# Eight plain chunks instead of six, one tile pair of weight forms a chunk, and packing spread over four steps

## The chip, the cores and the metric

The kernel runs on one core of one Trainium2 chip. The core has a matrix engine (PE, with its weight loads shown as PEld), a vector engine (DVE), a scalar engine (ACT), a general engine (POOL) and a queue that issues transfers (SP). Each runs its own instructions strictly in the order in which they stand; they wait for one another by semaphores. The metric is the time of one execution in microseconds of the device. Before the change the runs shown gave 1952.1, 1952.52 and 1952.86 us.

## The reference

x has 8192 tokens of 448 values. A spectral layer (Fourier transform, a small complex MLP on four blocks of 112, inverse transform) is followed by a GEGLU layer, both behind a normalised and modulated input:

```python
x = x + ga * _A_ref(h, A_w1, A_b1, A_w2, A_b2)      # spectral layer
h = _layernorm(x, axis=-1) * (1 + cb) + sb
x = x + gb * _B_ref(h, B_w_gate, B_w_up, B_w_down)  # GEGLU

def _B_ref(x, w_gate, w_up, w_down):                # 448 -> 1792 -> 448
    return (_gelu(x @ w_gate) * (x @ w_up)) @ w_down
```

The change lies wholly in the second half, the inverse transform's last stage and the GEGLU.

## The kernel before

Up to about 386 us the kernel does the transforms and the spectral MLP and prepares weights. Then it goes through the 8192 tokens in 32 chunks of 256. For precision every operand of the GEGLU products is split into a high and a low 16-bit part, so each product is three matmuls.

**Plain chunks.** The first NSTD = 6 chunks, numbered 0 to 5, do the gate and up products plainly. A chunk has 14 steps, one for each 128 columns of the hidden layer; step k of chunk i is `gate_up(i, k)`: 20 matmuls of 256 columns on PE, and for two hidden tiles together a group of eight of half height. ACT then makes the GELU (L1154, tile gel) and DVE multiplies it with the up half out of PSUM (L1159, tile x), which frees the bank; POOL makes four sums (L1167 to L1170), ACT and DVE the high and low parts (L1178, L1179, tile ac). The eight tiles of PSUM that gate/up and the other products share turn over, so PE can be about two steps ahead of L1159. After step 2 of a chunk comes `down` of the chunk before (seven products, 147 matmuls, L1191 to L1193; its tail of additions runs on DVE and on POOL, L1205, L1206, L1234).

**The work beside them.** During chunk i the input of chunk i + 2 is made ready, in steps given by the table `hooks`: splitting the spectral data into parts (step 3: ACT, and POOL L115), the inverse (step 6: PE, L1018 to L1020), the residual (step 7: DVE L1029, POOL L1030), the statistics (8: DVE L1038, L1041), the reciprocal root (9 and 10: DVE L124 to L133), the norm (11 and 12: DVE L1067, L1068), packing (13: ACT and POOL), and in step 0 of the next chunk the transposing transfers (`turn`).

**Set chunks.** The other 26 chunks use a scheme with seven products in place of eight for gate and up, 546 matmuls of 128 columns (L1350). It needs the weights in seven sums and differences, the weight forms, again in high and low parts. They are made while the plain chunks run, for seven tile pairs (n = 0 to 6): `load_forms` fetches a pair (four transfers, tile wr), `form_sums` makes the sums on POOL (L1528 to L1532, tiles wr and wf), `forms_hi` the high parts on ACT (L1557, tile ws), `forms_lo` the low ones on DVE (L1561), and `store_forms` copies three of them (POOL, L1566) and writes the pair to memory in two parts of four transfers (L1569). The set chunks then load them part by part (`load_part`, L1269) into the four slots that the plain weights leave.

A planner sets the place of this: `plan` gives each item a due time in microseconds (33 a pair, `spots` being the expected times of a chunk's steps), and an item comes at the first spot at or after it. So the pairs do not keep step with the chunks: about 1.4 of them fall to a chunk, each in four bursts of two or three pieces on ACT and DVE.

**The passage.** The last plain chunks also pack the inputs of the first two set chunks, which is more work: sums over the two token halves (`token_sums`: DVE L1294 to L1300) and five packings (`wpack_hi` on ACT, L1321, `wpack_lo` on POOL, L1327). In the kernel before all of it comes in step 13 (`pack`). The PSUM tiles of the set chunks (`sets`) take the place of those of the plain ones, so the first set matmul waits for the last L1159.

Of the kernel before, what the change touches and what calls it, by code (L numbers as in the profile page):

```python
# [40 lines left out]
NSTD = 6  # L41
# [8 lines left out]
def spectral_geglu(ctx, tc, x, w1, b1, w2, b2, wg, wu, wd, cvec, wmod, cf1, cs2, cmi, cgm, out):  # L50
# [924 lines left out]
    with ExitStack() as cctx:  # L975
# [558 lines left out]
        def form_cuts(t, part):  # L1534

            w, r, s2 = raws[("s", t, part // 2)], raws[("w", t)], raws[("f", t)].rearrange("p (c x) -> p c x", c=3)
            tq = r[:, :, 6:7]
            cuts = [
                [(A12, 0, r[:, 0, 3:6]), (A12, 3, tq[:, 0]), (A11, 0, r[:, 0, 0:3])],
                [(S1, 0, r[:, 1, 0:3]), (S2, 0, s2)],  # L1540
                [(A22, 0, r[:, 1, 3:6]), (S4, 3, tq[:, 0]), (S4, 0, r[:, 0, 3:6])],
                [(S3, 0, s2), (A22, 3, tq[:, 1].to_broadcast([128, 2, 128]))],
            ][part]
            f0 = WPARTS[part // 2][0]

            def out(l, f, c, src):
                if c == 0:
                    return w[:, l, 0:3, f - f0]
                return w[:, l, 3, f - f0 : f - f0 + src.shape[1]]

            return [(out(0, *cut), out(1, *cut), cut[2]) for cut in cuts]

        def forms_hi(t, part):
            if part % 2 == 0:
                raws[("s", t, part // 2)] = cp2.tile([128, 2, 4, 4 - part // 2, 128], F16, tag=f"ws{part}", name="ws")
            for hi, _, src in form_cuts(t, part):
                S.activation(hi, src, AF.Copy, scale=sww)  # L1557

        def forms_lo(t, part):
            for hi, lo, src in form_cuts(t, part):  # L1560
                V.scalar_tensor_tensor(lo, src, sww, hi, op0=ALU.mult, op1=ALU.subtract)  # L1561

        def store_forms(t, part):
            w = raws.pop(("s", t, part))
            if part == 0:
                G.tensor_copy(w[:, :, 3, 0:3], w[:, :, 2, 0:3])  # L1566
# [4 lines left out]
        spots = [(0, 2.4), (1, 4.9), (2, 7.3), ("m0", 11.3), ("m1", 13.3), ("m2", 17.4)]  # L1571
        spots += [(k, 21.4 + 2.44 * (k - 2)) for k in range(3, NFT)]
        prep = {}

        def plan(us, fn, *args):
            i, r = divmod(us, 48.2)
            i, p = next(((1 + int(i), p) for p, at in spots if at >= r), (2 + int(i), 0))
            prep.setdefault((i, p), []).append((fn, *args))

        for n in range(NP):  # L1580
            for us, fn, *args in (
                (0, load_forms),
                (11, form_sums, 0),
                (11, forms_hi, 0),
                (11, forms_lo, 0),
                (14, forms_hi, 1),
                (14, forms_lo, 1),
                (17, form_sums, 1),
                (19, store_forms, 0),
                (20, forms_hi, 2),  # L1590
                (20, forms_lo, 2),
                (23, forms_hi, 3),
                (23, forms_lo, 3),
                (28, store_forms, 1),
            ):
                plan(33 * n + us, fn, n, *args)
        for n, k in enumerate((4, 7, 11, 13)):
# [4 lines left out]
            0: [(1, turn)],  # L1602
# [228 lines left out]
```

## Time and profile before

| what | value |
|---|---|
| median of the runs shown | 1952.52 us |
| the profiled execution, and its span | 1953.62 us, 1951.8 us |
| PE, DVE, ACT, POOL busy | 96%, 74%, 52%, 65% of the span |
| mean granted clock of PE | 0.981 |
| plain chunks 1 to 5 begin and end | 425.98 us and 726.77 us |
| first set chunk ends, one later one | 778.05 us, 46.20 us long |

A row of the busy time by stage gives the stretch in us from the span's start, its length, then for each engine the busy time and the number of instructions, and last the granted clock of PE, the share of DMA time and GB/s. A row of a timeline gives start, length, engine, line, operation, the tiles written and read, and in brackets how long the engine stood idle before it and who ended that. A row of the groups gives busy time and mean length in ns, then the idle time before the group's instructions by who ended it. Matmuls overlap, so a matmul's length is more than what it adds.

### The profile page before, as it was taken

To read this page: it belongs to the slowest core of one execution; us is meant where nothing else is said; L and a number is where in the kernel's file an instruction comes from. 1 tells how busy PE (TensorE), PEld (TensorE's weight loads), DVE (VectorE), ACT (ScalarE), POOL (GpSimd) and SP (SyncE) were. 2 spreads that over 40 slices of the span, in tenths; PEclk is the share of its full clock that TensorE was granted. 3 is DMA by queue.
4 is the path that set the end of the run, shared out by engine and by line. 5 is a ranking of instruction groups with operands and counts; after the bars stand their busy time and mean duration, and the time that the engine had idled before them with its cause. 6 is when DMAs were issued, how large, how long until landed. Compare 5 with 4: busy or idle time off the path is not lost.

```text
span 1951.8 us, 57569 instructions
## 1 busy us (share of the span) xinstructions
PE 1867.3 (96%) x23808; PEld 1767.8 (91%) x23808; DVE 1451.8 (74%) x2919; ACT 1010.4 (52%) x1879; POOL 1276.7 (65%) x1633
## 2 busy tenths in 40 slices
PE   7899999899989859999999999999999999999998
PEld 3599999777878749999999999999999999999998
DVE  8677788786756666777777777777777777777745
ACT  5687788553433424555444444455455555545443
POOL 3157655256767666777777677777777777777633
PEclk9899999999989979999999999999999999999999
DMA  9999777654354466666666665666666655666561
GB/s 354 317 280 261 193 191 190 175 137 108 94 132 107 96 218 164 173 175 177 178 182 178 172 165 163 163 168 182 173 182 173 162 163 163 178 171 182 147 173 53
DMA packets 395454, 342.14 MB, mean 175 GB/s; under 512 B 113332, under 2 KB 373560, under 8 KB 395192
## 3 DMA queue, kind: packets, MB, share of 16 engines
q1 hardware_dynamic: 395192, 338.47, 62.8%
q8 instruction: 186, 3.05, 0.7%
q14 instruction: 76, 0.62, 0.1%
HBM read 254.33 MB, written 60.10 MB: 161 GB/s over the span
## 4 chain that ended last, share of the span: by engine, by line
PE 71%; DVE 10%; POOL 6%; DMA 5%; issue 3%; ACT 2%; SPq 2%; ACTq 0%; POOLq 0%; DVEq 0%
PE set L1350 40%; PE pdn L1193 5%; PE pdn L1191 5%; PE pdn L1192 5%; PE ps L210 2%; PE set L1193 2%; PE set L1191 2%; PE set L1192 2%; DVE y L471 1%; PE pgu L1118 1%; DMA wr<-in_B_w_up 1%; DVE ws L1561 1%; POOL x L1167 1%; DMA raw<-in_B_w_up 1%; SPq L1569 1%
## 5 line engine op out<-in xcount | busy, mean ns | idle before, releaser
L1350 PE MATMUL set<-nt,wk 128*128 128x128 f16 x14196 | 805.9, 219 | 7.5 <-ACT sb L1378 3.5
L1350 PEld LDWEIGHTS <-wk 128*128 128x128 f16 x14196 | 798.4, 98 | 12.9 <-issue 10.7
L1193 PE MATMUL pdn<-wd,ac 128*128 128x224 f16 x1190 | 308.3, 259 | 3.0 <-DVE ac L1179 1.8
L1191 PE MATMUL pdn<-wd,ac 128*128 128x224 f16 x1190 | 308.5, 259 | 2.3 <-DVE u L1227 0.7
L1192 PE MATMUL pdn<-wd,ac 128*128 128x224 f16 x1190 | 308.2, 259 | 0.0
L1399 ACT ACTIVATE gl<-c,dg 128x384 f32<-128x384 f32 x182 | 112.2, 616 | 275.5 <-DVE c L1393 274.4
L1425 DVE SCALAR_TENSOR_TENSOR ac<-x,sa_act,ac 128x896 f16<-128x896 f32 x182 | 229.6, 1261 | 16.1 <-ACT ac L1415 16.0
L1118 PE MATMUL pgu<-nt,wk 128*128 128x256 f16 (+1 forms) x1848 | 214.1, 282 | 16.2 <-DVE x L1159 16.2
L1118 PEld LDWEIGHTS <-wk 128*128 128x128 f16 (+1 forms) x1848 | 175.3, 101 | 54.7 <-issue 30.3
L1234 POOL TENSOR_TENSOR o<-u,p 128x224 f32<-128x224 f32 x32 | 21.0, 658 | 285.2 <-DVE u L1233 285.2
L1403 DVE TENSOR_TENSOR x<-c,gl 128x384 f32<-128x384 f32 x182 | 191.5, 1052 | 18.5 <-ACT gl L1399 18.5
L1167 POOL TENSOR_TENSOR x<-x 128x128 f32<-128x128 f32 x223 | 126.9, 569 | 118.7 <-DVE x L1159 50.2
L1415 ACT ACTIVATE ac<-x,sa_act 128x896 f16<-128x896 f32 x182 | 188.2, 1034 | 3.4 <-DVE x L1170 0.4
L1170 POOL TENSOR_TENSOR x<-x 128x128 f32<-128x128 f32 x223 | 175.5, 787 | 0.0
L1191 PEld LDWEIGHTS <-ac 128*128 128x128 f16 x1568 | 153.4, 98 | 6.6 <-issue 5.2
L1193 PEld LDWEIGHTS <-ac 128*128 128x128 f16 x1568 | 153.4, 98 | 4.2 <-DVE ac L1179 2.5
L1387 DVE TENSOR_TENSOR c<-set,sb 128x512 f32<-128x512 f32 x182 | 124.5, 684 | 43.6 <-PE set L1350 43.6
L1192 PEld LDWEIGHTS <-ac 128*128 128x128 f16 x1568 | 153.4, 98 | 1.8 <-issue 1.8
L1169 POOL TENSOR_TENSOR x<-x 128x128 f32<-128x128 f32 x223 | 147.5, 661 | 0.0
L1378 ACT COPY sb<-set 128x512 f32<-128x512 f32 x182 | 105.0, 577 | 54.5 <-PE set L1350 54.5
L471 DVE SCALAR_TENSOR_TENSOR y<-pm,t 64x224 f32<-64x224 f32 x256 | 99.5, 389 | 39.0 <-ACT t L463 35.1
L115 POOL TENSOR_TENSOR yl<-y,yh 128x448 fp32r<-128x448 f32 x63 | 76.6, 1215 | 73.7 <-ACT yh L113 58.1
(323 smaller groups left out, 3993.5 us busy)
## 6 DMA issues: line engine op xcount, KB each, us to landing
wk<-wk SPq DMA_DIRECT2D x82, 1024.0 KB, 5.6
wk<-wk SPq DMA_DIRECT2D x82, 768.0 KB, 10.5
tr<-td SPq DMA_DIRECT2D x64, 224.0 KB, 4.7
vd<-us SPq DMA_DIRECT2D x64, 224.0 KB, 3.1
xx<-in_A_x SPq DMA_DIRECT2D x32, 448.0 KB
v<-vd SPq DMA_DIRECT2D x63, 224.0 KB, 6.3
out<-x SPq DMA_DIRECT2D x31, 448.0 KB, 5.3
xt<-in_A_x SPq DMA_DIRECT2D x15, 896.0 KB, 16.3
```

The lines of the kernel that those rows point to most:

```text
L1118: T.matmul(pgu[i, t, q][:, pr * H : (pr + 1) * H], ws[rows, n, w, tw], nts[i][rows, tn, :], start=start, stop=stop, skip_group_check=True,)
L1167: e.tensor_tensor(s1, a21, a22, ALU.add)
L1169: e.tensor_tensor(s3, a11, a21, ALU.subtract)
L1170: e.tensor_tensor(s4, a12, s2, ALU.subtract)
L1191: T.matmul(ps, ac[:, 0, ka], w[:, 0, kb], start=n == 0, stop=False)
L1192: T.matmul(ps, ac[:, 0, ka], w[:, 1, kb], start=False, stop=False)
L1193: T.matmul(ps, ac[:, 1, ka], w[:, 0, kb], start=False, stop=n == NP - 1)
L1350: T.matmul(ps2[:, pr, reg * 128 : reg * 128 + 128], slot[:, pr, hl, wt, :], nt[:, xt, :], start=start and j == 0, stop=j == len(terms) - 1 ...
L1387: V.tensor_tensor(c[:, :, 1:3, :], p[:, :, 0:256].rearrange("p g (r c) -> p g r c", r=2), b[:, :, 0:128].rearrange("p g (o c) -> p g o c", ...
L1403: V.tensor_tensor(xs[u][:, 1::3, :], cts.pop(u)[:, 1], gls.pop(u), ALU.mult)
L1415: S.activation(ac[:, 0], xs[u][:, 0:7], AF.Copy, scale=sa_act[:, t : t + 1])
L1425: V.scalar_tensor_tensor(ac[:, 1], xs.pop(u)[:, 0:7], sa_act[:, t : t + 1], ac[:, 0], op0=ALU.mult, op1=ALU.subtract)
```

## The change

NSTD becomes 8, so two set chunks become plain ones (6 and 7), and there are seven plain chunks, 1 to 7, for the seven tile pairs: pair n belongs to chunk n + 1. The planner with its due times goes. A table names, for every step of a chunk (m0, m1, m2 are places inside the down), what is done of the chunk's pair. The pieces are numbered 0 to 9; DVE's low part of a piece stands a step behind ACT's high part. The second sums on POOL come in step 7, ahead of the residual. A pair is loaded in step 13 of the chunk before; its parts are stored in steps 8 and 13. The copy of three forms goes from POOL (in `store_forms`) to DVE (in `forms_lo`, after piece 4). `turn` goes from step 0 to step 5, the output's store from step 5 to step 4. In chunks 6 and 7, which prepare chunks 8 and 9, a second table `soon` takes the place of `hooks`: the reciprocal root, the norm and the token sums each come one to three steps earlier, and the packing comes in pieces in steps 10 to 13.

Chunk 3, DVE, from the residual of step 7 to the reciprocal root of step 9 (x with pi and ga_r is the residual, cst and cmv the statistics, x with pgu and gel the draining of a bank). Before:

```order
L1029 TENSOR_TENSOR x_5747<-pi_8289,ga_r 128x448
L1029 TENSOR_TENSOR x_5747<-pi_8293,ga_r 128x448
L1159 TENSOR_TENSOR x_8365<-pgu,gel 128x2x128
L1038 BN_STATS cst_8372<-x_5747 128x6 x2
L1041 BN_AGGR cmv<-cst_8372 128x2 x2
L1159 TENSOR_TENSOR x_8365<-pgu,gel 128x2x128
L1179 SCALAR_TENSOR_TENSOR ac<-x_8327,sa_act,ac 128x896
L124 TENSOR_SCALAR rcve<-cmv 128x2
```

After, the same place:

```order
L1029 TENSOR_TENSOR x_5747<-pi_8227,ga_r 128x448
L1029 TENSOR_TENSOR x_5747<-pi_8231,ga_r 128x448
L1159 TENSOR_TENSOR x_8307<-pgu,gel 128x2x128
L1561 SCALAR_TENSOR_TENSOR ws<-wr,sww,ws 128x3x128
L1038 BN_STATS cst_8316<-x_5747 128x6 x2
L1041 BN_AGGR cmv<-cst_8316 128x2 x2
L1159 TENSOR_TENSOR x_8307<-pgu,gel 128x2x128
L1179 SCALAR_TENSOR_TENSOR ac<-x_8265,sa_act,ac 128x896
L1561 SCALAR_TENSOR_TENSOR ws<-wr,sww,ws 128x128
L1561 SCALAR_TENSOR_TENSOR ws<-wr,sww,ws 128x256
L124 TENSOR_SCALAR rcve<-cmv 128x2
```

Three form pieces (5, 6 and 7) now stand between; two more follow in steps 11 and 12.

Chunk 3, POOL, the sums of step 7 and what follows. Before:

```order
L1167 TENSOR_TENSOR x_8327<-x_8327 128x128
L1168 TENSOR_TENSOR x_8327<-x_8327 128x128
L1169 TENSOR_TENSOR x_8327<-x_8327 128x128
L1170 TENSOR_TENSOR x_8327<-x_8327 128x128
L1030 TENSOR_TENSOR x_5747<-x_5747,xx 128x448 x2
L1167 TENSOR_TENSOR x_8365<-x_8365 128x128
```

After:

```order
L1167 TENSOR_TENSOR x_8265<-x_8265 128x128
L1168 TENSOR_TENSOR x_8265<-x_8265 128x128
L1169 TENSOR_TENSOR x_8265<-x_8265 128x128
L1170 TENSOR_TENSOR x_8265<-x_8265 128x128
L1525 TENSOR_TENSOR wr<-wr,wf 128x384
L1526 TENSOR_TENSOR wf<-wr,wf 128x384
L1030 TENSOR_TENSOR x_5747<-x_5747,xx 128x448 x2
L1167 TENSOR_TENSOR x_8307<-x_8307 128x128
```

The pair's second sums have come between the step's own sums and the residual's additions.

The last plain chunk, DVE, from the norm to the last drain (tf are the token sums). Before, chunk 5:

```order
L1067 SCALAR_TENSOR_TENSOR n_9947<-x_5746,cmv,cb_r 128x448
L1068 SCALAR_TENSOR_TENSOR n_9947<-n_9947,rcy,sb_r 128x448
L1159 TENSOR_TENSOR x_9972<-pgu,gel 128x2x128
L1067 SCALAR_TENSOR_TENSOR n_9947<-x_5746,cmv,cb_r 128x448
L1068 SCALAR_TENSOR_TENSOR n_9947<-n_9947,rcy,sb_r 128x448
L1159 TENSOR_TENSOR x_9972<-pgu,gel 128x2x128
L1179 SCALAR_TENSOR_TENSOR ac<-x_9933,sa_act,ac 128x896
L1294 TENSOR_TENSOR tf<-n_9947 128x192
L1295 TENSOR_TENSOR tf<-n_9947 128x192
```

After, chunk 7:

```order
L1294 TENSOR_TENSOR tf<-n_11181 128x192
L1295 TENSOR_TENSOR tf<-n_11181 128x192
L1159 TENSOR_TENSOR x_11250<-pgu,gel 128x2x128 x2
L1179 SCALAR_TENSOR_TENSOR ac<-x_11111,sa_act,ac 128x896
L1561 SCALAR_TENSOR_TENSOR ws<-wr,sww,ws 128x3x128
L1298 TENSOR_TENSOR tf<-n_11181,tf 128x192
L1299 TENSOR_TENSOR tf<-n_11181,tf 128x192
L1300 TENSOR_TENSOR tf<-n_11181 128x64
L1159 TENSOR_TENSOR x_11293<-pgu,gel 128x2x128
L1561 SCALAR_TENSOR_TENSOR ws<-wf,sww,ws 128x3x128
L1159 TENSOR_TENSOR x_11293<-pgu,gel 128x2x128
```

The token sums have moved from behind the last drain to ahead of the last three steps' drains, among form pieces.

```diff
-NSTD = 6
+NSTD = 8
...
         def pack(i):
-            if i < NSTD:
-                pack_hi(i)
-                pack_lo(i)
-            else:
-                for part in range(2):
-                    token_sums(i, part)
-                wpack_hi(i, range(5))
-                wpack_lo(i, range(5))
+            pack_hi(i)
+            pack_lo(i)
...
-        def forms_hi(t, part):
-            if part % 2 == 0:
-                raws[("s", t, part // 2)] = cp2.tile([128, 2, 4, 4 - part // 2, 128], F16, tag=f"ws{part}", name="ws")
-            for hi, _, src in form_cuts(t, part):
+        def forms_hi(t, *ns):
+            for n in ns:
+                if n % 5 == 0:
+                    raws[("s", t, n // 5)] = cp2.tile([128, 2, 4, 4 - n // 5, 128], F16, tag=f"ws{n}", name="ws")
+                hi, _, src = form_cut(t, n)
                 S.activation(hi, src, AF.Copy, scale=sww)
 
-        def forms_lo(t, part):
-            for hi, lo, src in form_cuts(t, part):
+        def forms_lo(t, *ns):
+            for n in ns:
+                hi, lo, src = form_cut(t, n)
                 V.scalar_tensor_tensor(lo, src, sww, hi, op0=ALU.mult, op1=ALU.subtract)
+                if n == 4:
+                    w = raws[("s", t, 0)]
+                    V.tensor_copy(w[:, :, 3, 0:3], w[:, :, 2, 0:3])
 
         def store_forms(t, part):
             w = raws.pop(("s", t, part))
-            if part == 0:
-                G.tensor_copy(w[:, :, 3, 0:3], w[:, :, 2, 0:3])
...
         for n in range(NP):
-            for us, fn, *args in (
+            for k, fn, *args in (
                 (0, load_forms),
-                (11, form_sums, 0),
-                (11, forms_hi, 0),
...
-                (28, store_forms, 1),
+                ("m0", form_sums, 0),
+                ("m0", forms_hi, 0),
+                ("m1", forms_lo, 0),
...
+                (7, form_sums, 1),
+                (7, forms_hi, 5),
+                (8, forms_lo, 5),
+                (8, forms_hi, 6, 7),
+                (8, store_forms, 0),
+                (9, forms_lo, 6, 7),
+                (10, forms_hi, 8),
+                (11, forms_lo, 8),
+                (11, forms_hi, 9),
+                (12, forms_lo, 9),
+                (13, store_forms, 1),
             ):
-                plan(33 * n + us, fn, n, *args)
+                at_k = (n, NFT - 1) if k == 0 and n else (1 + n, k)
+                prep.setdefault(at_k, []).append((fn, n, *args))
...
         hooks = {
-            0: [(1, turn)],
+            5: [(1, turn)],
...
+        soon = {
+            5: [(1, turn)],
+            3: [(2, split_g), (2, split_v)],
+            6: [(2, inverse)],
+            7: [(2, residual)],
+            8: [(2, stats2), (2, rsqrt_part, 5)],
+            9: [(2, rsqrt_part, 9), (2, norm2, 0)],
+            10: [(2, norm2, 1), (2, token_sums, 0), (2, wpack_hi, [0, 1]), (2, wpack_lo, [0, 1])],
+            11: [(2, token_sums, 1), (2, wpack_hi, [2]), (2, wpack_lo, [2])],
+            12: [(2, wpack_hi, [3]), (2, wpack_lo, [3])],
+            13: [(2, wpack_hi, [4]), (2, wpack_lo, [4])],
         }
...
-                if k == 5:
+                if k == 4:
                     store_out()
...
-                for d, fn, *args in hooks.get(k, []):
+                for d, fn, *args in (hooks if i < NSTD - 2 else soon).get(k, []):
```

More of the change, by code (lines that the diff above doesn't have):

```diff
@@ L1532, in form_sums, with form_cut @@
                 G.tensor_tensor(s2, a22, s2, ALU.subtract)
-        def form_cuts(t, part):
-            w, r, s2 = raws[("s", t, part // 2)], raws[("w", t)], raws[("f", t)].rearrange("p (c x) -> p c x", c=3)
+        def form_cut(t, n):
+            w, r, s2 = raws[("s", t, n // 5)], raws[("w", t)], raws[("f", t)].rearrange("p (c x) -> p c x", c=3)
             tq = r[:, :, 6:7]
[L1538 to L1551, printed above, removed]
@@ L1553, in forms_hi @@
[L1553 to L1556 removed]
+            f, c, src = [
+                (A12, 0, r[:, 0, 3:6]),
+                (A12, 3, tq[:, 0]),
+                (A11, 0, r[:, 0, 0:3]),
+                (S1, 0, r[:, 1, 0:3]),
+                (S2, 0, s2),
+                (A22, 0, r[:, 1, 3:6]),
+                (S4, 3, tq[:, 0]),
+                (A22, 3, tq[:, 1].to_broadcast([128, 2, 128])),
+                (S4, 0, r[:, 0, 3:6]),
+                (S3, 0, s2),
+            ][n]
```

28 lines of the change are left out of this document (13 added, 15 removed).

## The prediction

> **What bounds the kernel now.** I read the page first (span, slices), then the busy time by stage, then the timelines of PE and DVE inside single chunks. Two lines of the page:
>
> ```profile
> span 1951.8 us, 57569 instructions
> PE   7899999899989859999999999999999999999998
> ```
>
> PE is the bound in the long second half, where every slice stands at 9. The change touches slices 9 to 17, where PE falls to 8 and once to 5. Next the engines' busy time by stage: plain chunks 1 to 5, each cut at its first gate/up matmul, the first set chunk, and one undisturbed set chunk.
>
> ```profile
> core 0: us, PE busy (x) PEld busy (x) DVE busy (x) ACT busy (x) POOL busy (x), PEclk, DMA share, GB/s
> 425.98:483.53 57.55, 52.93 (x463) 45.33 (x462) 41.00 (x84) 21.75 (x41) 37.01 (x44) 0.94 0.49 119
> 483.53:537.08 53.55, 49.46 (x467) 43.32 (x464) 39.13 (x70) 23.39 (x44) 42.76 (x50) 1.00 0.36 87
> 537.08:596.54 59.46, 53.48 (x459) 45.68 (x459) 36.21 (x62) 20.71 (x37) 38.18 (x47) 0.89 0.53 131
> 596.54:652.76 56.22, 49.53 (x467) 43.11 (x465) 37.17 (x68) 24.44 (x46) 43.13 (x50) 1.00 0.32 76
> 652.76:726.77 74.01, 55.50 (x459) 46.45 (x459) 43.34 (x75) 23.45 (x46) 42.94 (x54) 0.84 0.65 177
> 726.77:778.05 51.28, 47.73 (x699) 47.20 (x699) 33.02 (x68) 21.81 (x44) 35.48 (x49) 0.97 0.72 190
> 778.05:824.25 46.20, 46.16 (x702) 45.66 (x700) 36.10 (x69) 22.95 (x44) 34.51 (x46) 1.00 0.66 172
> ```
>
> In the second column a plain chunk takes 54 to 74 us, a set chunk 46.20. What a plain chunk takes with nothing in its way comes from pieces of chunk 2 (two steps; three steps with one group of half-height matmuls; one down product; one inverse) and, last, step 0 of chunk 1.
>
> ```profile
> 506.75:511.12 4.37, 4.37 (x43) 3.92 (x42) 1.36 (x3) 1.99 (x4) 4.21 (x5) 1.00 0.84 235
> 506.75:513.94 7.19, 7.19 (x71) 6.10 (x69) 2.34 (x3) 2.55 (x5) 6.96 (x9) 1.00 0.93 233
> 492.47:506.75 14.28, 14.27 (x150) 14.01 (x148) 8.74 (x14) 4.29 (x9) 9.95 (x14) 1.00 0.52 117
> 516.12:517.49 1.37, 1.37 (x9) 0.89 (x7) 1.37 (x2) 1.16 (x3) 1.37 (x2) 1.00 0.00 0
> 425.98:429.68 3.70, 3.70 (x26) 2.65 (x25) 2.70 (x4) 2.23 (x5) 2.30 (x4) 1.00 0.03 7
> ```
>
> A step is 4.37/2 = 2.18, a half-height group 7.19 - 4.37 - 2.18 = 0.64, so a clean chunk is 14 x 2.18 + 3.5 x 0.64 + 14.28 + 1.37 = 48.4 us. Chunks 1 to 5 lose 300.8 - 5 x 48.4 = 58.8 us. PE's timeline shows where; the bracket names who ended the wait before the row.
>
> ```profile
> 489.87 2.77 PE L1118 MATMUL pgu<-nt,wk 64*128 64x256 f16 x25 [1.49 <-DVE x L1159]
> 536.67 4.55 PE L1118 MATMUL pgu<-nt,wk 64*128 64x256 f16 x26 [2.43 <-DVE x L1159]
> 693.87 0.74 PE L1019 MATMUL pi<-vh,gl 128*128 128x448 f32 x1 [8.22 <-POOL gl L115]
> 696.85 0.74 PE L1020 MATMUL pi<-v,gh 128*128 128x448 f32 x1 [2.24 <-POOL v L115]
> 726.77 1.44 PE L1350 MATMUL set<-nt,wk 128*128 128x128 f16 x23 [2.47 <-DVE x L1159]
> ```
>
> There are two kinds of wait. The inverse waits for POOL's low parts (L115), which stand behind form work; and gate/up waits until DVE has drained a PSUM bank (L1159), which stands behind form pieces and the next chunk's normalisation. The ACT group of form pieces shows the first kind from its other side: 41.4 us idle in front of them, half of it for POOL's sums.
>
> ```profile
> L1557 ACT ACTIVATE ws<-wr,sww 128x384 f16<-128x384 f32 x35 | 21.3, 609 | 41.4 <-POOL wr L1531 21.7 <-DMA wr<-in_B_w_up 14.0 <-POOL wr L1528 5.8
> L1561 DVE SCALAR_TENSOR_TENSOR ws<-wr,sww,ws 128x384 f16<-128x384 f32 x35 | 32.7, 935 | 16.9 <-ACT ws L1557 16.8
> L1566 POOL COPY ws<-ws 128x768 f16<-128x768 f16 x7 | 7.4, 1063 | 0.0
> ```
>
> **The sum's frame.** Chunk 0 and all from the fourth set chunk on stay as they are. From 425.98 to the end of the third set chunk the kernel now spends 57.55 + 53.55 + 59.46 + 56.22 + 74.01 + 51.28 + 2 x 46.20 = 444.5 us. After the change the same work is plain chunks 1 to 7 and one set chunk. Two set chunks turned plain cost 2 x (48.4 - 46.20) = 4.4; if all were clean it would be 7 x 48.4 + 46.2 = 385, a gain of 59. The question is what stays dirty.
>
> **Steps 3 to 6.** There is now one tile pair a chunk instead of about 1.4, its second sums stand behind the split (step 7), and the copy L1566 goes from POOL to DVE. Ahead of the inverse POOL keeps only the down's tail and the split, so chunk 5's waits of 8.22 + 2.24 and their like in chunks 1 and 3 go: I take 0 left, between 0 and the 2.24 of the last low part. The cover is POOL's tail ending in time. The copy on DVE has no row; it costs between 0 and 1.06 at step 6, where DVE has room, so nothing. On SP a pair's four loads go to step 13 of the chunk before, behind four stores that wait for DVE's last piece, and are wanted only in the down; the four transposes go from step 0 to 5, past the loads of v and g, which no longer queue behind them; the output store goes from step 5 to 4, ahead of the form stores. I cost these at nothing, covered by the 14.28 of the down; if loads land late, up to 1 us a chunk.
>
> **Steps 7 to 13.** Here DVE is nearly full even without forms. Chunk 3 had none in these steps; its step 7 ended on PE at 582.78. The last three rows are POOL's second sums and, of chunk 2, DVE's ten pieces in its steps 6 to 10.
>
> ```profile
> 587.99 0.63 DVE L1038 BATCH_NORM_STATS2 cst<-x 128x6 f32<-128x448 f32 x1 [0.87 <-POOL x L1030]
> 596.00 0.88 DVE L1067 SCALAR_TENSOR_TENSOR n<-x,cmv,cb_r 128x448 f32<-128x448 f32 x1
> 596.92 0.76 DVE L1068 SCALAR_TENSOR_TENSOR n<-n,rcy,sb_r 128x448 f32<-128x448 f32 x1
> 597.94 0.95 DVE L1067 SCALAR_TENSOR_TENSOR n<-x,cmv,cb_r 128x448 f32<-128x448 f32 x1
> 598.92 0.69 DVE L1068 SCALAR_TENSOR_TENSOR n<-n,rcy,sb_r 128x448 f32<-128x448 f32 x1
> 599.53 0.42 DVE L1159 TENSOR_TENSOR x<-pgu,gel 128x256 f32<-128x256 f32 x1
> 527.12 1.01 POOL L1531 TENSOR_TENSOR wr<-wr,wf 128x384 f32<-128x384 f32 x1
> 528.21 1.00 POOL L1532 TENSOR_TENSOR wf<-wr,wf 128x384 f32<-128x384 f32 x1
> 517.50:535.00 17.50, 6.33 (x10) 1.00 0.10 23
> ```
>
> The drain of step 13 ended at 599.95, 17.2 us after step 7; PE needs it in the next chunk's step 1, 8 x 2.18 + 0.64 = 18.1 after: 0.9 spare (0.6 in an even chunk, where step 2 needs it). The change puts ahead of it POOL's second sums, which hold back the residual's adds and with them the statistics (528.21 + 1.00 - 527.12 = 2.1; piece 5 fits into the 0.87 wait), and pieces 6 to 9 at 6.33/10 = 0.63, together 2.5. I take 0.63 because it is from the same place in a chunk; the 0.935 of the group, with its collisions, is the upper end (3.7), and a lower one is 3.0 in all, if the sums overlap with DVE's backlog. DVE is late by 4.6, PE loses 3.7 (odd) or 4.0 (even): a chunk of 52.1 or 52.4, and chunk 1, with the 3.70 - 2.18 of its step 0, 53.6.
>
> **The clock.** After the wait at 489.87 the granted clock (the third number from the end) stayed at 1.00; around the one at 536.67 it was 0.76.
>
> ```profile
> 485.71:495.00 9.29, 7.80 (x77) 6.67 (x75) 8.08 (x12) 5.51 (x9) 6.99 (x9) 1.00 0.04 9
> 533.97:541.00 7.03, 4.60 (x27) 3.17 (x27) 6.72 (x17) 1.44 (x3) 3.60 (x4) 0.76 0.83 214
> ```
>
> In an odd chunk the loss comes in lots of 0.8 to 1.8, nearer the first row: nothing. In an even one the first lot, at step 13, is 2.1 + 1.3 - 0.9 = 2.5, as in the second row: 7.03 x 0.24 = 1.7, so 54.1. The Trainium skill, TensorE: Matmul & The Clock Gate (Why this matters for your kernels), says to keep PE's idle gaps under about 3 us. By it even chunks would stay warm too and the sum be 3.4 lower; the second row, cold after 2.43, speaks against it, and I keep the charge.
>
> **The passage.** In chunks 6 and 7 the new table does statistics to packing some steps earlier. Two rows for the token sums:
>
> ```profile
> 727.69 0.61 DVE L1294 TENSOR_TENSOR tf<-n 128x192 f32<-128x192 f32 x1
> 728.76 0.60 DVE L1298 TENSOR_TENSOR tf<-n,tf 128x192 f32<-128x192 f32 x1
> ```
>
> In chunk 6 both norms (0.88 + 0.76 + 0.95 + 0.69 = 3.3) and two sums (1.2) now stand ahead of the drain of step 11, on which step 13 waits: 2.1 + 1.3 + 3.3 + 1.2 - 0.9 = 7.0, and one or two cold stretches, 2.5: 57.9. In chunk 7 all token sums (2 x 0.61 + 0.60, and 0.8 put for the two smaller ones: 2.6) stand ahead of step 13's drain, for which the first set matmul waits (as at 726.77): 17.2 + 4.6 + 2.6 = 24.4 after step 7, where PE is done at 13.7. That is 10.7 of idling and a chunk of 59.1, against 74.01 now. The set chunk behind it stays at 51.28 and starts colder, 1.7: 53.0.
>
> **Sum.** 53.6 + 2 x 54.1 + 2 x 52.1 + 57.9 + 59.1 + 53.0 = 436.0, against 444.5: -8.5 us. The profiled execution took 1953.62 for a span of 1951.8; the median of the runs shown is 1952.52, so I forecast 1952.5 - 8.5 = 1944 us. A measurement of this kernel tells about 0.2%, 3.9 us, from no change. The dear end: 1.2 more for the pieces (7.2 in six chunks), cold stretches in chunks 1, 3 and 5 too (5.1), late loads (6): 1962.
>
> **Rivals.** (a) DVE keeps up, since pieces spread singly fall into its own small gaps: chunks 1 to 5 at 50.0 (-16.4), chunk 6 at 52 (-5.9), the passage 3 shorter: 1919. For it: chunk 2 came to 53.55 with ten pieces crowded there. Against: the spare 0.9. (b) Slower: POOL's sums in step 7 and DVE's pieces lengthen each other, the waits all grow past 2.43, and the half clock follows: chunks 1 to 6 at 57.5, as chunk 1 now: 6 x 57.5 + 112.1 - 444.5 = +12.6, 1965. It decides from a mean of (444.5 - 112.1)/6 = 55.4 upward. The Trainium skill, SBUF — State Buffer (Who interferes with whom), has DVE and GpSimd share one port pair as an exclusive lock, which is this way of getting longer; 0.935 in the group against 0.63 in the row from chunk 2 agrees that pieces can stretch. (c) The passage isn't shortened: the wk loads, which SP issues ahead of the output store, hold that store and the residual that writes its buffer; chunk 7 takes 74 again: 1959. (d) The spreading doesn't free the inverse: some 4 us of waiting stay in chunks 1, 3 and 5: 1956.
>
> **Chances.** The forecast 0.45, (a) 0.18, (b) 0.19, (c) 0.10, (d) 0.08. Faster is most of the forecast and (a): 0.60; within 0.2% the forecast's rest and the milder half of (c) and (d): 0.16; slower 0.24. The range 1917 to 1962 leaves out most of (b)'s upper half and (a)'s edge; the forecast's own is 1932 to 1954.
>
> **What would show it.** Right: no wait of the inverse on POOL above 2.2 us; PE waiting 3 to 5 us a chunk for L1159, around steps 11, 13 and the next 0 to 2; the first set matmul waiting some 10 us for L1159. Wrong: plain chunks of 50 or of 57, the tile loads landing after the down's first products, or POOL's tail reaching step 6.

## The result

The changed kernel takes 1933.39 us (median of 4 runs, 1932.38 to 1934.26), the kernel before 1952.69 beside it: 19.3 us less, a ratio of 0.9900 with a 95% interval of 0.9883 to 0.9917. The forecast was 1944, 8.5 us less: the right side, inside the range, but less than half of the gain. The profiled execution of the changed kernel took 1934.03 us.

The page of the kernel after, the 40 slices of PE (the span is 1931.7 us):

```profile
PE   7899999899999999799999999999999999999998
```

The dent of slice 15 (a 5) has become a 7, two slices later. Busy time by stage, cut as before at each chunk's first gate/up matmul: plain chunks 1 to 7 and the first set chunk. After the start and end come the length, then the busy time and count of PE, PE's weight loads, DVE, ACT and POOL, then the granted clock, the DMA share and GB/s.

```profile
426.75:477.82 51.07, 50.08 (x464) 43.79 (x463) 37.13 (x81) 20.03 (x37) 34.74 (x41) 1.00 0.31 80
477.82:529.61 51.79, 49.29 (x465) 43.23 (x465) 31.93 (x63) 20.12 (x37) 36.64 (x45) 1.00 0.38 94
529.61:580.15 50.54, 48.68 (x458) 42.98 (x458) 30.85 (x61) 20.04 (x36) 35.96 (x44) 1.00 0.38 96
580.15:631.95 51.80, 49.31 (x466) 43.26 (x465) 31.95 (x63) 20.24 (x37) 36.66 (x45) 1.00 0.38 94
631.95:682.48 50.53, 48.67 (x458) 43.00 (x458) 30.86 (x61) 20.04 (x36) 35.77 (x44) 1.00 0.39 96
682.48:738.06 55.58, 49.77 (x465) 43.46 (x465) 35.58 (x69) 20.99 (x39) 38.04 (x48) 0.98 0.37 88
738.06:798.12 60.06, 50.63 (x459) 44.27 (x458) 37.47 (x75) 23.47 (x45) 42.57 (x57) 0.93 0.71 195
798.12:850.22 52.10, 48.97 (x700) 48.44 (x699) 30.97 (x63) 20.71 (x41) 31.71 (x43) 0.94 0.80 203
```

Together 423.5 us, where the prediction had 436.0 and the kernel before 444.5. Chunks 1 to 5 are even now, and the clock stays at 1.00 to the end of chunk 5. PE's timeline from chunk 4's begin to the first set matmul has these waits among those that are left, with their releaser in the bracket; in the whole of it no row of the inverse waits. The group of all gate/up matmuls (busy time, mean ns, then all idle time ahead of them and who ended it) stands behind it.

```profile
586.37 0.81 PE L1118 MATMUL pgu<-nt,wk 64*128 64x256 f16 x7 [1.37 <-DVE x L1159]
...
631.53 4.96 PE L1118 MATMUL pgu<-nt,wk 64*128 64x256 f16 x45 [0.93 <-DVE x L1159]
...
637.29 2.34 PE L1118 MATMUL pgu<-nt,wk 128*128 128x256 f16 x20 [0.80 <-DVE x L1159]
...
734.99 0.27 PE L1118 MATMUL pgu<-nt,wk 64*128 64x256 f16 x1 [1.34 <-DVE x L1159]
...
737.33 9.74 PE L1118 MATMUL pgu<-nt,wk 64*128 64x256 f16 x65 [2.08 <-DVE x L1159]
...
798.12 3.22 PE L1350 MATMUL set<-nt,wk 128*128 128x128 f16 x32 [8.08 <-DVE x L1159]
```

```profile
L1118 PE MATMUL pgu<-nt,wk 128*128 128x256 f16 (+1 forms) x2464 | 274.6, 275 | 19.0 <-DVE x L1159 18.9
```

So the inverse is free, as forecast, and all of gate/up's 19.0 us of waiting is for DVE's drains (L1159). Why DVE is late is seen on POOL and DVE behind step 7 of chunk 3: POOL makes the pair's second sums first (L1525, and L1526 right behind it) and the residual's adds (L1030) after them, and the statistics (L1038) wait 1.98 us.

```profile
569.22 0.99 POOL L1525 TENSOR_TENSOR wr<-wr,wf 128x384 f32<-128x384 f32 x1
...
571.45 2.22 POOL L1030 TENSOR_TENSOR x<-x,xx 128x448 f32<-128x448 f32 x2
...
572.61 0.63 DVE L1038 BATCH_NORM_STATS2 cst<-x 128x6 f32<-128x448 f32 x1 [1.98 <-POOL x L1030]
```

### The profile page after: what moved, and what is told of

The parts are those of the page before. It is cut to its first block, busy times and chain, and to the rows that moved or that the text cites. A ratio compares the mean times of both kernels' runs of the same rounds, so it can differ in the third digit from the quotient of the medians.

```text
span 1931.7 us, 56478 instructions
## 1 busy us (share of the span) xinstructions
PE 1862.0 (96%) x23332; PEld 1757.8 (91%) x23332; DVE 1417.0 (73%) x2888; ACT 995.3 (52%) x1843; POOL 1261.5 (65%) x1616
## 4 chain that ended last, share of the span: by engine, by line
PE 72%; DVE 14%; DMA 4%; ACT 4%; POOL 3%; issue 2%; SPq 1%; ACTq 0%; POOLq 0%; DVEq 0%
PE set L1350 36%; PE pdn L1193 6%; PE pdn L1191 6%; PE pdn L1192 6%; PE pgu L1118 4%; PE ps L210 2%; PE set L1193 2%; PE set L1192 2%; PE set L1191 2%; DVE y L471 2%; DVE ws L1561 1%; DVE ac L1179 1%; DVE x L1159 1%; POOL x L1030 1%; DVE wk L824 1%
## 5 line engine op out<-in xcount | busy, mean ns | idle before, releaser
L1350 PE MATMUL set<-nt,wk 128*128 128x128 f16 x13104 | 745.4, 219 | 12.7 <-DVE x L1159 8.1
L1350 PEld LDWEIGHTS <-wk 128*128 128x128 f16 x13104 | 738.3, 98 | 17.9 <-issue 15.9
L1193 PE MATMUL pdn<-wd,ac 128*128 128x224 f16 x1218 | 315.5, 259 | 1.7 <-DVE ac L1425 1.2
L1191 PE MATMUL pdn<-wd,ac 128*128 128x224 f16 x1218 | 315.7, 259 | 0.8 <-ACT ac L1415 0.6
L1192 PE MATMUL pdn<-wd,ac 128*128 128x224 f16 x1218 | 315.5, 259 | 0.0
L1118 PE MATMUL pgu<-nt,wk 128*128 128x256 f16 (+1 forms) x2464 | 274.6, 275 | 19.0 <-DVE x L1159 18.9
L1118 PEld LDWEIGHTS <-wk 128*128 128x128 f16 (+1 forms) x2464 | 227.1, 98 | 65.1 <-issue 38.5
L1425 DVE SCALAR_TENSOR_TENSOR ac<-x,sa_act,ac 128x896 f16<-128x896 f32 x168 | 212.5, 1265 | 14.8 <-ACT ac L1415 14.7
L1167 POOL TENSOR_TENSOR x<-x 128x128 f32<-128x128 f32 x223 | 135.4, 607 | 122.0 <-DVE x L1159 82.9
L1403 DVE TENSOR_TENSOR x<-c,gl 128x384 f32<-128x384 f32 x168 | 176.2, 1049 | 17.1 <-ACT gl L1399 17.1
L1415 ACT ACTIVATE ac<-x,sa_act 128x896 f16<-128x896 f32 x168 | 173.7, 1034 | 3.5 <-DVE x L1170 0.4
L1170 POOL TENSOR_TENSOR x<-x 128x128 f32<-128x128 f32 x223 | 171.3, 768 | 0.0
L1169 POOL TENSOR_TENSOR x<-x 128x128 f32<-128x128 f32 x223 | 146.3, 656 | 0.0
L1387 DVE TENSOR_TENSOR c<-set,sb 128x512 f32<-128x512 f32 x168 | 115.0, 685 | 42.5 <-PE set L1350 42.5
L1168 POOL TENSOR_TENSOR x<-x 128x128 f32<-128x128 f32 x223 | 117.3, 526 | 17.5
## 6 DMA issues: line engine op xcount, KB each, us to landing
xt<-in_A_x SPq DMA_DIRECT2D x15, 896.0 KB, 16.4
```

Source lines behind the costliest of these rows:

```text
L1118: T.matmul(pgu[i, t, q][:, pr * H : (pr + 1) * H], ws[rows, n, w, tw], nts[i][rows, tn, :], start=start, stop=stop, skip_group_check=True,)
L1167: e.tensor_tensor(s1, a21, a22, ALU.add)
L1169: e.tensor_tensor(s3, a11, a21, ALU.subtract)
L1170: e.tensor_tensor(s4, a12, s2, ALU.subtract)
L1191: T.matmul(ps, ac[:, 0, ka], w[:, 0, kb], start=n == 0, stop=False)
L1192: T.matmul(ps, ac[:, 0, ka], w[:, 1, kb], start=False, stop=False)
```

## The experiments

The change has at least five parts: one pair a chunk (eight plain chunks), pieces spread over the steps, the copy on DVE, new places for turn and the output store, and a second table for the passage. The first four experiments take them apart.

### e1: the count alone

From the kernel before:

```diff
-NSTD = 6
+NSTD = 8
...
-                plan(33 * n + us, fn, n, *args)
+                plan(48.2 * n + us, fn, n, *args)
```

> The kernel before with eight plain chunks instead of six and one tile pair a chunk (pitch 48.2 us instead of 33), its planner, its four lumps of pieces, POOL's copy, its passage and its places for turn and the output store all kept. Theory (the gain has two parts, fewer pairs a chunk and their spreading): all pieces of a pair fall between the down and step 4, so steps 7 to 13 hold none and nothing waits there for DVE, but the second sums, the copy and the split stand in one row on POOL ahead of the inverse, which waits 2 to 4 us in every plain chunk: chunks 1 to 6 at 51 to 52.5, chunk 7 near 74, a sum over chunks 1 to 7 and the first set chunk of some 436, 1944 us. Rival (the spreading does it, the count nothing): chunks stay near the 60.2 of now, 1965 us or more. Rival (the count does it all): 1933 us.

Measured: 1930.09 us (ratio 0.9879, 0.9864 to 0.9894), 22.7 less than the kernel before. These two lines give the whole gain, by the medians 3 us more (the two intervals overlap); the theory's 1944 is far off, and the rival that gave it all to the count (1933) came nearest. The two lines do two things at once: a chunk has fewer pairs, and the pairs keep step with the chunks. No run parts the two. Chunks 3 and 7 by stage:

```profile
531.99:582.05 50.06, 48.29 (x458) 43.04 (x458) 34.20 (x62) 20.37 (x37) 38.31 (x46) 1.00 0.39 97
...
732.64:793.57 60.93, 50.88 (x460) 43.96 (x459) 37.84 (x73) 23.57 (x46) 42.81 (x54) 0.94 0.56 165
```

In the timeline, the end of POOL's row ahead of the inverse and the inverse's wait, both in chunk 4, then chunk 7's SP queue (issues; a row of SPq lasts from the first of its issues to the end of the last) and its residual:

```profile
610.82 1.15 POOL L1566 COPY ws<-ws 128x768 f16<-128x768 f16 x1
...
612.80 2.08 POOL L115 TENSOR_TENSOR v<-v,vh 128x896 fp32r<-128x896 f32 x1
...
614.94 0.47 PE L1020 MATMUL pi<-v,gh 128*128 128x448 f32 x1 [1.57 <-POOL v L115]
...
752.14 12.80 SPq L1569 DMA_DIRECT2D wk<-ws  x4
...
773.08 1.73 SPq L1677 DMA_DIRECT2D out<-x  x1
...
779.71 1.16 DVE L1029 TENSOR_TENSOR x<-pi,ga_r 128x448 f32<-128x448 f32 x2 [6.86 <-DMA out<-x]
```

The reader sees two things. With one pair in a chunk, its four lumps all fall between the down and step 5, where DVE has room: in chunks 3 to 6 PE waits for no drain behind step 7, and the inverse waits 1.56 to 1.75 us in every chunk, where in the kernel before it lost 4 to 10 us in chunks 1, 3 and 5. The pairs' loads are in time too: in the kernel before POOL's first sums waited 18.3 us for them, in chunks 3 and 5, and in e1 not at all. So a plain chunk takes 50.2 (mean of chunks 3 to 6), less than the 51.2 of the kernel after (chunks 2 to 5), which has no wait of the inverse but longer ones behind step 7. And in chunk 7 the four stores of a pair's first part hold SP for 12.80 us, since one of them waits 10.1 us for POOL's copy L1566 and the next stand behind it; the output store stands behind them, 40.4 us into the chunk, and the residual waits 6.86 us for it.

### e2: no second table

From the kernel after (pack as before, for set chunks with token sums and their packing at step 13):

```diff
-(hooks if i < NSTD - 2 else soon).get(k, [])
+hooks.get(k, [])
```

> The kernel after without its second table: chunks 6 and 7 go through statistics and norm at the steps of all others, and the packing for the set chunks stands at step 13 in one lump, as before. Theory (the early packing is worth what the prediction said): chunk 6 shrinks to the 51.8 of chunk 4, chunk 7 with its first set matmul goes from 60.1 to 74, the first set chunk stays: 177 against 167.7, +9, 1943 us. Rival (chunk 7 was long before because of the inverse's 10.5 us and the output store's 7.2, which the other parts have removed, not because of the packing): chunk 7 at 57, 1926 us.

Measured: 1926.73 us (ratio 0.9866, 0.9851 to 0.9881), 6.7 less than the kernel after: the rival. Chunks 6 and 7 by stage:

```profile
679.82:731.62 51.80, 49.31 (x465) 43.26 (x465) 31.94 (x63) 20.23 (x37) 36.65 (x45) 1.00 0.42 94
731.62:789.59 57.97, 48.86 (x458) 42.92 (x458) 38.61 (x76) 23.86 (x46) 41.92 (x53) 0.97 0.74 203
```

Packed late, chunk 6 is like chunk 4, and chunk 7 2.1 us shorter than with early packing. What the second table puts ahead of the drains (norms and token sums, which e2 doesn't part) made PE wait, and nobody needed it early.

### e3: turn and output store back

From the kernel after, the first edit in both tables:

```diff
-            5: [(1, turn)],
+            0: [(1, turn)],
...
-                if k == 4:
+                if k == 5:
                     store_out()
```

> The kernel after with the transposes' issue (turn) back at step 0 and the output store back at step 5, as before. Theory (both cost nothing, as the prediction had it): within 2 us of the kernel after, 1931 to 1936. Rival (at step 0 the four transposes wait on SP for POOL's packing and hold back the form loads and the loads of v and g behind them; the output store behind the form stores holds the residual): 1 to 2 us a chunk, 1941 to 1947.

Measured: 1932.43 us (0.9900, 0.9884 to 0.9917), against 1933.39 for the kernel after: no difference that could be told from none, as the prediction had it.

### e4: the second sums behind the residual

From the kernel after:

```diff
-                (7, form_sums, 1),
                 (7, forms_hi, 5),
+                (8, form_sums, 1),
```

> The kernel after with POOL's second sums of a pair one step later, at step 8, behind the residual's two adds and not ahead of them. Theory (the sums are the largest term of DVE's lateness, 2 of 4.0 us): statistics no longer wait 1.98 (odd) or 3.05 (even) for POOL, every drain behind them comes 1.9 earlier, the 2.75 us that a plain chunk loses after step 7 fall to about 0.9 in chunks 1 to 6, and chunk 7's first set matmul waits 6 instead of 8.1: 10 to 15 us in all, 1919 to 1923 us. Rival (the sums only move: on the port they lengthen DVE's rows as much where they now stand, or the pieces behind them come late): less than 4 us, 1930 to 1934.

Measured: 1923.91 us (0.9850, 0.9835 to 0.9865), 9.5 less than the kernel after, at the short end of the theory; the rival (under 4) is out. Chunks 3 and 4 by stage, then POOL and DVE in chunk 3's timeline:

```profile
525.77:575.02 49.25, 48.30 (x459) 42.97 (x458) 31.53 (x61) 20.24 (x36) 35.77 (x44) 1.00 0.40 99
575.02:625.27 50.25, 48.88 (x468) 43.27 (x465) 32.41 (x63) 20.25 (x37) 36.69 (x45) 1.00 0.39 97
```

```profile
565.27 2.54 POOL L1030 TENSOR_TENSOR x<-x,xx 128x448 f32<-128x448 f32 x2
...
566.74 0.61 DVE L1038 BATCH_NORM_STATS2 cst<-x 128x6 f32<-128x448 f32 x1
...
567.77 1.00 POOL L1525 TENSOR_TENSOR wr<-wr,wf 128x384 f32<-128x384 f32 x1
```

The adds come first, the statistics wait for nothing, and an odd and an even chunk together take 99.50 instead of 102.34: 1.4 us a chunk, less than the 1.98 that the statistics no longer wait. The four late pieces still stand ahead of the drains.

### e5 and e6: the count, with the copy on DVE, and with the output store at step 4

e5 is e1 with this, e6 is e5 with the store of outputs at step 4:

```diff
         def forms_lo(t, part):
...
+            if part == 1:
+                w = raws[("s", t, 0)]
+                V.tensor_copy(w[:, :, 3, 0:3], w[:, :, 2, 0:3])
...
         def store_forms(t, part):
-            if part == 0:
-                G.tensor_copy(w[:, :, 3, 0:3], w[:, :, 2, 0:3])
```

> The kernel of e1 (the kernel before with eight plain chunks and one pair a chunk, 1930.1 us) with the copy inside the stored tile on DVE, behind the lump with S2, instead of on POOL ahead of the split. Theory (POOL's row ahead of the inverse sets the wait that is left): the 1.15 us of the copy go from that row, the inverse's 1.57 to 1.75 fall to 0.4 to 0.6 in chunks 1 to 7: 7 x 1.15 = 8 us, 1922 us. Rival (the split waits for something else, or the copy on DVE delays the lump that holds the drains of steps 4 and 5): less than 3 us, 1927 to 1931.

> The kernel of e5 with the output store at step 4 instead of 5, ahead of the wk loads of chunk 7. Theory (in chunk 7 the output store stands on SP behind wk loads that wait, and the residual's first product waits 6.9 us for the tile that it reads): chunk 7 goes from 61 to some 55 and nothing else moves: 6 us less than e5, 1916 us. Rival (the first set matmul waits for DVE's norms and sums anyway): within 2 us of e5.

Measured: e5 1914.53 us (0.9806, 0.9792 to 0.9821), e6 1913.38 (0.9803, 0.9785 to 0.9820). One moved instruction brought 15.6 us, twice what the theory said. Of e5, chunk 7 by stage:

```profile
727.04:779.80 52.76, 48.29 (x460) 43.05 (x459) 37.07 (x72) 23.56 (x46) 40.56 (x51) 0.99 0.67 191
```

and in its timeline chunk 4's inverse, and SP's issues in chunk 7:

```profile
611.07 0.47 PE L1020 MATMUL pi<-v,gh 128*128 128x448 f32 x1 [0.85 <-POOL v L115]
...
745.34 3.34 SPq L1570 DMA_DIRECT2D wk<-ws  x4
...
760.68 0.57 SPq L1678 DMA_DIRECT2D out<-x  x1
```

The inverse's wait fell by 0.7 to 1.0, near the theory's 1.15, which is about 6 us over chunks 1 to 6. Chunk 7 gives 8.2 more (60.93 to 52.76): without the copy in POOL's row the four stores take SP 3.34 us instead of 12.80, the output store goes out 33.6 us into the chunk instead of 40.4, and the residual waits 0.84 for it instead of 6.86. That was the job that e6 was to do, and little of it was left: e6 is within 1.2 us of e5, as its rival said, but the reason that the rival gave is not tested by it.

### e7: both single gains in the kernel after

e2 and e4 together.

> The kernel after with both single gains: second sums at step 8 (e4, 9.5 us less than after) and one table for all chunks (e2, 6.7 less). Theory (they are separate: the one acts on DVE's backlog in every chunk, the other on chunks 6 to 8): 1933.4 - 9.5 - 6.7 = 1917 us, chunk 6 at 49.9, chunk 7 at 56. Rival (e2's gain came from the same backlog): 1922 to 1924.

Measured: 1918.79 us (0.9830, 0.9816 to 0.9845): the two gains add up but for 1.6 us (1917.2 by the sum). What still divides it from e5 and e6 (4 to 5 us) may be the four pieces behind step 7; no run moved them alone.

### e8: longer waits on purpose

From the kernel after:

```diff
+        def extra_rows(n):
+            for _ in range(n):
+                V.bn_stats(cp2.tile([128, 6], F32, tag="extra", name="extra"), gb_r)
+
+        for at_k, n in (((2, 10), 2), ((3, 10), 3), ((4, 10), 5), ((5, 10), 5)):
+            prep.setdefault(at_k, []).append((extra_rows, n))
```

> The kernel after with extra DVE rows (statistics of a constant row into a tile that nobody reads, 0.54 to 0.63 us each) at step 10: two in chunk 2, three in chunk 3, five in chunks 4 and 5, so that PE's waits for the drains of steps 11 to 13 grow by 1.1, 1.7 and 2.8 us. Theory from the traces so far (the clock is set anew every 3.41 us; it halves for the next 3.41 when PE idled over about 1.9 of the last ones, in one wait or in several; largest idle that stayed warm 1.83, least that went cold 2.02): each such window with 2.0 or more of idle is followed by a half clock and none with 1.8 or less, so chunks 4 and 5 go cold once or twice each, chunk 2 not; a wait of over 2.1 that two windows share may stay warm. Rival of the prediction (a single wait of about 2.4 or more decides): only those waits, and all of them. Rival (about 3 us): at most one of them. Time: 15 rows cost 8 to 9.5 us by their length, and each cold stretch up to 1.7 more: 1942 to 1952 us.

Measured: 1942.78 us (0.9956, 0.9939 to 0.9973), 9.4 more than the kernel after, for 15 rows of 0.62 us. Two of the waits in PE's timeline, in chunks 2 and 5, and the stretches of 3.4 us around each by the windows view (start and end, length, PE busy first, the clock the third number from the end):

```profile
530.27 8.76 PE L1118 MATMUL pgu<-nt,wk 64*128 64x256 f16 x65 [2.12 <-DVE x L1159]
...
692.82 4.85 PE L1118 MATMUL pgu<-nt,wk 128*128 128x256 f16 x43 [3.33 <-DVE x L1159]
```

```profile
526.80:530.30 3.50, 1.39 (x15) 0.83 (x14) 3.22 (x14) 1.28 (x2) 0.01 (x1) 1.00 0.00 0
530.30:533.70 3.40, 3.40 (x19) 2.19 (x19) 3.36 (x5) 0.84 (x2) 3.32 (x4) 0.51 0.02 5
...
687.40:690.80 3.40, 2.09 (x20) 1.73 (x18) 3.23 (x9) 1.55 (x2) 0.00 (x0) 1.00 0.00 0
690.80:694.20 3.40, 1.38 (x13) 1.24 (x13) 3.16 (x13) 0.84 (x2) 1.03 (x1) 1.00 0.01 2
694.20:697.60 3.40, 3.40 (x32) 2.68 (x31) 3.37 (x6) 0.78 (x1) 2.51 (x4) 1.00 0.02 5
```

A wait of 2.12 us that lies in one window halved the clock for the next 3.4 us; one of 3.33 that two windows share (1.31 and 2.02 idle) did not. No bound on the length of a single wait, 2.4 or 3 us, can tell these two apart. In chunk 4 a wait of 4.10 was followed by a half clock. The theory was off all the same: it had chunk 2 warm and chunk 5 cold, since where the windows lie was not known, and by its bound of 2.0 the window with 2.02 should have gone cold.

### e9 and e10: the copy, back in the kernel after and alone in the kernel before

e9 is the kernel after with `G.tensor_copy` where it has `V.tensor_copy`; e10 is the kernel before, six plain chunks, with the diff of e5.

> The kernel after with the copy inside the stored tile back on POOL (at step 6, behind the split in its row). Theory (the copy cost 16 us in e1 because it stood ahead of the split and of the stores that SP's row waits for; in the changed kernel's place POOL is free for 1.9 us behind it): within 3 us of the kernel after, 1931 to 1936. Rival (it costs by its length wherever it stands, by way of POOL's second sums and the residual): 7 x 1.1 = 8 us more, 1941.

> The kernel before, six plain chunks, with nothing changed but the copy on DVE instead of POOL. Theory (the copy ahead of the split is a good part of what chunks 1, 3 and 5 lose): each of seven copies takes 1.1 us off the inverse's waits, and in chunk 5 the store of the first part goes out earlier, so that the output store behind it on SP no longer holds the residual (7.2 us): 10 to 15 us less, 1936 to 1942. Rival (with 1.4 pairs a chunk the lumps of pieces on ACT and DVE set the waits): less than 4 us.

Measured: e9 1934.50 us (0.9907, 0.9892 to 0.9922), no different from the kernel after. e10 1944.82 (0.9959, 0.9944 to 0.9974), 7.9 less than the kernel before: between theory and rival. So the copy costs by where it stands in the rows of POOL and SP, not by its length: 15.6 us in e1, 7.9 in the kernel before, nothing in the kernel after, where it stands behind the split. The part of the theory that held is the store: chunk 5's residual, which waited 7.22 us for the output store, waits no more. First the kernel before, then e10:

```profile
712.91 1.16 DVE L1029 TENSOR_TENSOR x<-pi,ga_r 128x448 f32<-128x448 f32 x2 [7.22 <-DMA out<-x]
```

```profile
702.69 1.15 DVE L1029 TENSOR_TENSOR x<-pi,ga_r 128x448 f32<-128x448 f32 x2
```

The part that failed is the inverse: in chunk 5 it waits as long as before. e10's timelines of the four engines show why:

```profile
674.06 1.41 ACT L1557 ACTIVATE ws<-wr,sww 128x384 f16<-128x384 f32 x3 [9.01 <-DMA wr<-in_B_w_up]
...
674.71 2.92 DVE L1561 SCALAR_TENSOR_TENSOR ws<-wr,sww,ws 128x384 f16<-128x384 f32 x3 [5.59 <-ACT ws L1557]
...
678.37 0.66 POOL L1234 TENSOR_TENSOR o<-u,p 128x224 f32<-128x224 f32 x1 [1.42 <-DVE u L1233]
...
689.23 1.04 POOL L115 TENSOR_TENSOR gl<-g,gh 128x256 fp32r<-128x256 f32 x1
...
690.33 0.74 PE L1019 MATMUL pi<-vh,gl 128*128 128x448 f32 x1 [8.03 <-DMA wk<-ws]
```

The bracket of the last row names a store of forms, but the wait ended just after gl was there (689.23 + 1.04 = 690.27). Read from the top, the chain is this: the pair's loads come late; ACT waits 9.01 us for them; DVE's first pieces wait for ACT, and the down's last drains (L1232, L1233) stand behind these pieces on DVE; POOL's tail of the down waits for a drain, and from 678.37 on POOL runs without a pause through the tail, the four sums and the second sums to gl. So what chunk 5 lost at the inverse came first of all from a pair that was loaded in the chunk that used it, behind the five transposes on SP. It is the same in the kernel before, where the copy in this chunk stands behind the split.

### e11 and e12: what a clean chunk takes

e11 is e6 with the split of v in the down:

```diff
-            3: [(2, split_g), (2, split_v)],
+            3: [(2, split_g)],
...
+            if n == 1 and i + 2 < nch:
+                split_v(i + 2)
```

> The kernel of e6 (1913.4 us) with the split of v in the down, behind its third product, where POOL is idle for 4.5 us, instead of at step 3. Theory (what is left of the inverse's wait, 0.73 to 0.87 a chunk, is POOL's row): the wait goes, 7 x 0.8 = 5.6 us, 1908 us. Rival (v has not landed by then, or the split holds back POOL's part of the down): same or slower, 1912 to 1920.

Measured: 1906.99 us (0.9768, 0.9753 to 0.9784), the theory's number. Chunks 3, 4 and 7 by stage, then the two waits of the passage in PE's timeline:

```profile
529.30:577.17 47.87, 47.87 (x460) 43.14 (x458) 30.46 (x61) 20.46 (x37) 35.33 (x44) 1.00 0.42 102
577.17:625.65 48.48, 48.48 (x467) 43.35 (x464) 32.11 (x63) 19.99 (x36) 36.73 (x46) 1.00 0.41 100
722.00:773.34 51.34, 48.03 (x459) 43.14 (x458) 36.25 (x72) 23.75 (x46) 40.73 (x51) 1.00 0.67 199
```

```profile
773.34 3.46 PE L1350 MATMUL set<-nt,wk 128*128 128x128 f16 x32 [3.31 <-DVE x L1159]
...
778.80 8.76 PE L1350 MATMUL set<-nt,wk 128*128 128x128 f16 x154 [1.99 <-ACT sb L1378]
```

PE is busy for the whole of chunks 2 to 6. It is the fastest of all that were tried: 45.8 us under the kernel before and some 26 under the kernel after.

e12 is e11 with chunk 9's norm in chunk 7 behind step 13's drain:

```diff
+                    if i == NSTD - 1 and fn is norm2:
+                        continue
+                    if i == NSTD - 1 and fn is pack:
+                        norm2(i + d, 0)
+                        norm2(i + d, 1)
```

> The kernel of e11 (1907.0 us) with the norm of chunk 9, which stands in chunk 7 at steps 11 and 12, behind the drain of step 13, just ahead of its packing. Theory (in chunk 7 the first set matmul waits for whatever DVE has ahead of the last drain, and packing work may come late there): 3.3 us of norm leave DVE's row ahead of that drain, the wait of 3.31 falls to 0 to 0.6, and the one of 1.99 for ACT stays: 1903.5 to 1904.5 us. Rival (PE then waits as long for the next thing, the set chunk's first transposes or its PSUM copies): 1906 to 1908.

Measured: 1909.26 us (0.9772, 0.9757 to 0.9787): no gain, and by the trace 3.3 us more up to the end of the first set chunk. Again the two waits of the passage:

```profile
770.89 1.95 PE L1350 MATMUL set<-nt,wk 128*128 128x128 f16 x32 [1.02 <-DVE x L1159]
...
780.45 9.76 PE L1350 MATMUL set<-nt,wk 128*128 128x128 f16 x147 [7.61 <-ACT sb L1378]
```

The first wait fell from 3.31 to 1.02, and the second grew from 1.99 to 7.61: the norm now stands ahead of the packing, ACT casts what the norm leaves, and the PSUM copy that PE waits for stands behind those casts on ACT. That is the rival, somewhat dearer than it said.

## Why the prediction fell short

The direction and the places of the waits were right. What failed is the size of three terms, which together were charged 12.5 us too much: DVE's lateness in steps 7 to 13, the half clock of the even chunks, and the passage. They follow in the order of the prediction.

**Clean chunk (48.4).** Right: 47.87 and 48.48 in e11, 48.18 in the mean.

**Steps 3 to 6 (inverse waits to 0, the rest costed at nothing).** Right in what it said of the changed kernel: no row of the inverse waits, and e3 and e9 price turn, output store and copy at nothing there. It gave three reasons in one breath (one pair a chunk, second sums behind the split, the copy off POOL) and weighed none. e1 weighs the first, with the pairs in step: by itself it leaves 1.56 to 1.75 us a chunk of the inverse's waits and brings the whole gain. By e5 the copy is worth another 0.7 to 1.0 of these waits. The place of the second sums can then free the inverse of no more than the 0.73 to 0.86 that e5 leaves in chunks 2 to 7, and costs 1.4 a chunk in step 7 (e4). Two things were overlooked. The prediction's line of ACT's form pieces has 14.0 us for the pairs' loads beside the 21.7 for POOL's sums, and only the sums were read: the loads are where chunk 5's long wait begins (e10). And POOL's copy, through SP's stores, was part of what chunk 5 lost before.

**Steps 7 to 13 (DVE late, PE loses 3.7 or 4.0).** Right mechanism, and the places are those named: steps 11, 13 and the next 0 to 2. The size was too large. Against e11 the odd chunk loses 50.54 - 47.87 = 2.7 and the even one 51.80 - 48.48 = 3.3. By e4 the sums make 1.4 a chunk of it, where their 2.1 were charged in full. By subtraction that leaves some 1.6 for the four pieces, where 2.5 were charged; no run moved them alone. One reason is in the trace: the norm of the second half took 0.67 us in the kernel after, where the prediction carried on 0.95, so a late DVE made up some time:

```profile
533.17 0.67 DVE L1067 SCALAR_TENSOR_TENSOR n<-x,cmv,cb_r 128x448 f32<-128x448 f32 x1
```

In chunks 1 to 5 the forecast is 6.9 us too long by this term (2.5 + 0.6 + 1.6 + 0.6 + 1.6, without the clock's).

**The clock (1.7 in each even chunk).** Wrong, 3.4 us. It went by one wait of 2.43 us; the even chunks' loss came as waits of 0.93 and 0.80 that no window summed to 2, and the clock stayed at 1.00. In chunk 6 the wait of 1.34 and the first 0.7 of the next, of 2.08, fell into one window and the clock did halve, though neither was as long as 2.43; the cold stretch then lay mostly in chunk 7's first step, which fits that chunk 6 was 2.3 too long in the forecast and chunk 7 1.0 too short.

**The passage (57.9, 59.1, 53.0).** Near in size: 55.58, 60.06, 52.10, in part because a chunk too long and one too short offset each other. What the prediction left out is the comparison: it charged what the second table puts ahead of the drains and never asked what the passage takes without that table. By e2 it takes 6.7 us less. The last plain chunk was long before not because it packs late (chunk 7 of e2 does so too and takes 57.97) but because of the inverse's wait and of stores that wait for a copy with an output store behind them (e5, e10). Rival (c) looked at that store but held loads to blame; in the changed kernel chunk 7 takes 60.06 and not its 74.

**Rivals (a), (b), (d).** (b) is refuted: nothing grew past 2.43 in chunks 1 to 5. (d) is refuted for the changed kernel; in e1 it is the case, with 1.6 a chunk. (a) has chunks of 50.0 where 51.2 were measured: DVE keeps up half-way. (By its own chunk times (a) should have -16.0 and not -16.4 there.)

**The signs named at the end.** PE idles 1.9 us in an odd and 2.5 in an even chunk (its length less PE's busy time), where 3 to 5 were to show the forecast right; the first set matmul waits 8.08, where some 10 were named. One sign of being wrong came true: POOL's first sums wait 11.8 us in all for the pairs' loads, which land after the down's first products. It cost PE nothing that its timeline shows.

Sum of it: 12.5 us of the stages' 436.0 were not spent, 6.9 by DVE's term, 3.4 by the clock of the even chunks, and 2.2 in the passage.

## What to carry to other kernels

When a change has several parts, price the bluntest one, here how many pairs fall to a chunk and in what step, by itself before following the finer ones; the finer ones together brought nothing here. A short instruction on a shared row costs what stands behind it: follow it through the queue that its result releases (POOL's copy, SP's stores, the output store, the residual) and not by its length. Work that comes off the wait in front of one matmul and is put ahead of another's drain has only changed its creditor: what DVE and POOL do between a bank's last matmul and its drain is the dearest place in a chunk, and what nobody needs soon belongs behind it.

## What the runs showed of the hardware

The clock is granted in windows of 3.41 us that run on whatever the kernel does, and what counts is PE's idle time inside one window, in one wait or in several. Worked out from PE's rows and the clock's changes of all fourteen traces between 375 and 1870 us: of the windows at full clock, all 58 with 2.04 us or more of idle time were followed by a half clock, none of the more than 5900 with less than 1.65 was, and 2 of the 19 between were (at 1.69 and 2.02, while one at 2.03 stayed warm: the border isn't sharp in the traces). A half clock ended after every window with 0.34 us of idle time or less and never after one with more than 0.8. The Trainium skill, TensorE: Matmul & The Clock Gate (Part 1: The HAM clock gate), gives a free-running window of 3413 ns, which these traces agree with. The same page of the Trainium skill (Why this matters for your kernels) has the rule of no idle gaps over some 3 us between bursts of matmuls. These traces don't bear it out: 2.12 in one window went cold and 3.33 across two stayed warm.
